# Conditional weight splits as one branch per engine, queued behind the features, in a linear-attention and mixture-of-experts kernel

## The chip, the cores and the metric

The kernel runs on one core of a Trainium2 chip. The metric is the device time of one execution in microseconds (us). Engines: PE multiplies matrices and transposes, ACT applies functions and copies, DVE does elementwise work, POOL issues the gathers and scatters, SP issues the weight loads. Each engine takes its instructions in the order in which they are queued, and waits for another engine by semaphores.

## What is computed

A layer norm and linear attention with softmax features, then a layer norm and a mixture of 8 experts of which each token takes one, over 2048 tokens of width 512 (hidden width 1792). The change touches the second half:

```python
logits = xf @ w_gate
topk_idx = jnp.argsort(-logits, axis=-1)[:, :K]          # K = 1
gates = _softmax(topk_val, axis=-1)
for e in range(E):                                        # E = 8
    mask = (topk_idx == e)
    w = (gates * mask).sum(-1, keepdims=True)
    h = _silu(xf @ w1[e]) @ w2[e]
    out = out + w * h
```

All of it is in float32. A product of two float32 matrices is made of three passes over numbers that are split into a high and a low part: hi times hi, hi times lo, lo times hi (`mm3`, lines 89 to 92).

## The kernel before

Tokens are sorted by expert into blocks of 128. The second half runs units, one after the other, each for one expert:

- `unit0` (line 1263): the first block, of the expert with the most tokens in the first half. Its second product and the building of the block tables overlap.
- `pair(q)` (line 1323): two blocks, 256 tokens. Pairs 1 and 2 are always there; 3 to 8 stand in branches (line 1502) that are entered when there are enough blocks. Here pairs 1 to 4 run.
- `wide(w, hooks)` (line 1187): 288 tokens of one expert, twice, with the single blocks 0 and 1 (`single(r)`, line 1387) behind them.
- `single(r)`: one block of 128. Singles 2 to 7 stand in branches; here 2 and 3 run.

**Weights.** An expert has 7 chunks of 128 x 2048 numbers, 1 MB each: chunks 0 to 2 and half of 3 hold `w1`, the rest of 3 and 4 to 6 hold `w2`. SP loads a chunk to `raw[c]`. It is then split: ACT copies it to `whi[c]` (`hi_piece`, line 229; the copies are recorded at line 84), and DVE subtracts that from `raw[c]` to give `wlo[c]` (`lo_piece`, recorded at line 235). Either is done in halves of 128 x 1024. `split_chunk` does both halves, hi, lo, hi, lo. When both are done, `raw[c]` is loaded again for a later unit (`load`, or `fetch` in a branch on SP).

**Conditions.** A unit of the same expert as the one before needs no new weights. So `fls[u]` (a register on ACT and on DVE, from `load_fl`, line 1131) says whether unit u must split, and `flags[u]` (SP, line 1136) whether and what to load. `split(u, c)` (line 1152) has one branch, `tc.If(fls[u] > 0)`, around `split_chunk`, on two engines, and `fetch` behind it. In this run pairs 1 and 2 have the expert of unit0 and split nothing; pairs 3 and 4 and all later units have new weights.

**Steps.** A pair has 14 steps j over the hidden width. In each, PE makes g1 (12 products into `gw`), ACT the silu to `hs` and its high part, DVE its low part (both in `hA`, recorded at lines 84 and 87), and PE makes g2 of step j - 2 into `my`. `gw` is one tile of two halves, used in turn. At the end of step j the functions of `todo[j]` are called. `step(c, i, ...)` (line 1246) splits half i of chunk c, conditionally when it is for a pair, inside `with after(pin["hi"]), after(pin["lo"])`. `ahead` and `turned` norm a block of the next pair and turn its features (transposes on PE, high part on ACT, low part on DVE). A wide has the same steps with `hooks`.

**Order.** A planner at compile time chooses the order of the instructions on each engine, from their dependences and its own estimate of durations. `after(i)` (line 147) ties what is written inside it: those of its instructions that are on i's engine are queued behind i. A branch is placed as a whole, and the tie holds for a branch that is on that engine alone.

**Singles.** Each of four gemm1 groups (`mh`) is followed by a silu (line 220) and the transposes of the one before (`tr`, line 242); then come g2 (`yl` or `my`), the conditional splits of chunks 0 to 3 for the next single and, in their midst, that one's norm and transposes (line 1455). Single 1 also writes out the rows of wide 1 (`wide_out`), one tile of which lies in `raw[2]`, and refills chunks.

## Time and profile before

| | |
|---|---|
| median of 3 runs | 694.05 us (690.66 to 696.5) |
| the profiled execution | 695.41 us, span 693.7 us |
| mean granted clock of PE | 0.971 |
| attention and block tables | 0 to about 285 us of the span |
| pair 1, pair 2 | 285.1 to 338.1, to 389.3 |
| pair 3, pair 4 | to 432.6, to 476.5 |
| wide 0, single 0 | to 527.6, to 552.0 |
| wide 1, single 1 | to 600.2, to 634.1 |
| single 2, single 3 | to 665.7, to 687.3 |

The stages are read from the timeline of PE. In the timeline a row has the start, the length, the engine, the line, the operation, the tiles (out<-in), and in brackets the idle time of that engine just before and what ended it. "ACTq" and "DVEq" are the instruction sequencers of those engines: a wait for them is a wait for a branch. Lines of helpers stand for all their callers, so L84, L87 and L235 are told apart by their tiles: `hA` belongs to features of a step, `whi` and `wlo` to a split.

### The profile page before, as it was taken

What the parts mean: (1) busy time and instruction counts of PE and PEld (TensorE: products, weight loads), DVE (VectorE), ACT (ScalarE), POOL (GpSimd) and SP (SyncE); (2) the same over time, 40 slices, a digit from 0 to 9 for tenths busy, and PEclk for the clock granted to TensorE, in tenths of its full rate; (3) what the DMA queues carried; (4) which work ended last, traced back from release to release, by engine and by line L of the source; (5) the groups of instructions that cost most, each with busy time, mean ns of one, the idle gap of its engine ahead of it and who ended that gap; (6) DMA issues with size and microseconds to landing.
All of it is one profiled execution on the core that took longest, in us unless ns stands there. A gap on an engine that the chain in (4) does not pass through costs nothing. (4 is left out here: it accounts for less than half of the span.)

```text
span 693.7 us, 14767 instructions
## 1 busy us (share of the span) xinstructions
PE 641.8 (93%) x5455; PEld 566.2 (82%) x5455; DVE 454.3 (65%) x897; ACT 376.0 (54%) x674; POOL 239.0 (34%) x340
## 2 busy tenths in 40 slices
PE   9999999999999999789979899996999999949696
PEld 7888888888899987579868797895998899838484
DVE  7988877878988698613224656554658585844833
ACT  6566666675354475423234664664558386734641
POOL 5476788787165574200210200201203300142010
PEclk9999999999999999789999999999999999979989
DMA  9511111201023781660204563754645876565510
GB/s 330 189 48 47 52 57 47 62 19 32 18 78 123 276 303 64 241 258 1 66 18 134 175 242 112 254 183 152 223 159 201 296 257 222 194 255 204 193 49 19
DMA packets 25210, 101.53 MB, mean 146 GB/s; under 512 B 3326, under 2 KB 3326, under 8 KB 17056
## 3 DMA queue, kind: packets, MB, share of 16 engines
q1 hardware_dynamic: 21088, 88.15, 36.2%
q0 software_dynamic: 3888, 12.24, 5.4%
q8 instruction: 47, 0.77, 0.4%
q14 instruction: 43, 0.35, 0.1%
q10 hardware_dynamic: 144, 0.02, 0.0%
HBM read 91.98 MB, written 8.81 MB: 145 GB/s over the span
## 5 line engine op out<-in xcount | busy, mean ns | idle before, releaser
L235 DVE TENSOR_TENSOR wlo<-raw,whi 128x1024 fp32r<-128x1024 f32 (+1 forms) x130 | 151.8, 1188 | 84.7 <-ACT whi L84 80.0
L84 ACT ACTIVATE whi<-raw 128x1024 fp32r<-128x1024 f32 (+1 forms) x135 | 130.8, 999 | 34.7 <-DMA raw<-in_w_dram 17.3
L181 POOL DMA_INDIRECT out_dram<-xg,sidx x17 | 22.1, 1302 | 178.6 <-DVE xg L1239 140.8
L87 DVE TENSOR_TENSOR hA<-hs,hA 128x256 fp32r<-128x256 f32 (+1 forms) x84 | 36.3, 432 | 64.5 <-ACT hA L84 32.9
L90 PE MATMUL gw<-xhi,whi 128*128 128x256 f32 x224 | 66.6, 297 | 5.4 <-ACT hs L1373 3.4
L663 POOL TENSOR_TENSOR ph<-t,sm 128x1024 f32<-128x1024 f32 x32 | 62.1, 1940 | 19.5 <-DVE sm L661 19.3
L1373 ACT ACTIVATE hs<-gw 128x256 f32<-128x256 f32 x56 | 21.6, 385 | 85.6 <-PE gw L92 85.6
L92 PE MATMUL gw<-xhi,wlo 128*128 128x256 f32 x224 | 65.0, 290 | 2.3 <-DVEq L1153 2.3
L91 PE MATMUL gw<-xlo,whi 128*128 128x256 f32 x224 | 65.3, 292 | 0.0
L168 POOL DMA_INDIRECT xg<-hbuf,gidx x28 | 31.4, 1122 | 69.1 <-DMA out_dram<-xg,sidx 34.8
L92 PE MATMUL my<-whi,hA 128*128 128x512 f32 x122 | 49.1, 403 | 4.0 <-DVE hA L87 4.0
L660 DVE TENSOR_REDUCE sm<-t 128x64 f32<-128x1024 f32 x32 | 38.8, 1214 | 20.2 <-ACT t L655 18.3
L90 PEld LDWEIGHTS gw<-xhi,whi 128*128 128x128 f32 x224 | 44.3, 198 | 9.5 <-ACT hs L1373 4.9
L655 ACT ACTIVATE t<-t,rstd 128x1024 f32<-128x1024 f32 x32 | 36.8, 1150 | 27.3 <-DVE t L654 24.9
L90 PE MATMUL my<-whi,hA 128*128 128x512 f32 x122 | 49.1, 402 | 1.2 <-ACTq L1153 1.2
L91 PE MATMUL my<-wlo,hA 128*128 128x512 f32 x122 | 48.8, 400 | 0.4 <-DVEq L1153 0.4
L92 PEld LDWEIGHTS gw<-xhi,wlo 128*128 128x128 f32 x224 | 44.5, 199 | 2.5 <-DVEq L1153 2.5
L91 PEld LDWEIGHTS gw<-xlo,whi 128*128 128x128 f32 x224 | 44.4, 198 | 1.9
L90 PE MATMUL po<-wohi,xh 128*128 128x260 f32 x128 | 37.5, 293 | 1.3 <-DVE lg L918 1.3
L84 ACT ACTIVATE hA<-hs 128x256 fp32r<-128x256 f32 (+1 forms) x84 | 35.9, 427 | 3.1 <-ACTq L1250 0.4
L92 PE MATMUL po<-wohi,xl 128*128 128x260 f32 x128 | 36.5, 285 | 0.1
L91 PE MATMUL po<-wolo,xh 128*128 128x260 f32 x128 | 36.1, 282 | 0.0
(418 smaller groups left out, 1897.9 us busy)
## 6 DMA issues: line engine op xcount, KB each, us to landing
raw<-in_w_dram SPq DMA_DIRECT2D x63, 1024.0 KB, 5.3
xt<-in_x_dram SPq DMA_DIRECT2D x32, 256.0 KB, 2.7
hbuf<-hb SPq DMA_DIRECT2D x8, 515.0 KB, 3.5
xT<-in_xTs_dram SPq DMA_DIRECT2D x16, 256.0 KB, 2.7
phT<-in_wv_dram SPq DMA_DIRECT2D x4, 256.0 KB, 4.0
phT<-in_wqkT_dram SPq DMA_DIRECT2D x4, 256.0 KB, 4.9
phT<-in_wqkT_dram SPq DMA_DIRECT2D x2, 512.0 KB, 5.9
phT<-in_wo_dram SPq DMA_DIRECT2D x2, 512.0 KB, 7.7
```

The costliest lines, as they stand in the source:

```text
L84: return A.activation(dst, src, AF.Copy)
L87: return V.tensor_tensor(dst, src, hi.bitcast(F32), op=OP.subtract)
L90: T.matmul(ps, ahi, bhi, start=first, stop=False)
L91: T.matmul(ps, ahi, blo, start=False, stop=False)
L92: return T.matmul(ps, alo, bhi, start=False, stop=last)
L168: G.indirect_dma_start(out=dst[0:n, :], out_offset=None, in_=hbuf if col else hbuf[0:S // 2, :], in_offset=bass.IndirectOffsetOnAxis(ap=gi ...
L181: m = G.indirect_dma_start(out=out, out_offset=bass.IndirectOffsetOnAxis(ap=sidx[0:n, col:col + 1], axis=0), in_=src[0:n, 0:D], in_offset= ...
L235: return eng.tensor_tensor(lo, r, h.bitcast(F32), op=OP.subtract)
L655: pin["ex"] = A.activation(t, t, AF.Exp, scale=st[c]["rstd"])
L660: V.tensor_reduce(sm, t, AX.X, OP.add)
L663: pin["f2"] = G.tensor_tensor(ph.rearrange("p (a f) -> p a f", f=DH), t, bc(sm, DH), op=OP.mult)
L1373: A.activation(h, p, AF.Silu)
```

## The change

A split gets two branches: one on ACT with the high halves, one on DVE with the low halves, each on its own register. `step` uses the same for its half. `split` no longer fetches; `split_fetch` does both. In the diff the lines that only rename are left out:

```diff
-    fls = {}
+    fls = {ENG.Activation: {}, ENG.DVE: {}}
...
-    def split(u, c):
-        with tc.If(fls[u] > 0):
-            split_chunk(c)
+    def split(u, c, i0=0, i1=2):
+        with tc.If(fls[ENG.Activation][u] > 0):
+            for i in range(i0, i1):
+                hi_piece(c, i)
+        with tc.If(fls[ENG.DVE][u] > 0):
+            for i in range(i0, i1):
+                lo_piece(c, i)
+
+    def split_fetch(u, c):
+        split(u, c)
         fetch(u, c)
...
@@ step
                 if u is not None and u < NQ:
-                    with tc.If(fls[u] > 0):
-                        half(c, i)
+                    split(u, c, i, i + 1)
```

The tiles of a wide: norm (`tile_n`) and transposes (`tile_t`) are two functions. In `wide` the first step has a bank of its own in both wides, and each g1 is queued behind the one before:

```diff
-                p = (bank("mh") if j == w else gw[:, (j + w) % 2, :])[:, 0:WN]
+                p = (bank("mh") if j == 0 else gw[:, j % 2, :])[:, 0:WN]
...
+                    with after(pin["g1"] if j else None):
```

At the end of `unit0` one conditional split stays; the others, and the splits of chunks 5 and 6, go to pair 1:

```diff
-        for c in range(4):
+        for c in range(5):
             load(c, nx0)
-            split(1, c)
+        with after(xh), after(xl):
+            split_fetch(1, 0)
         result(0, py, xg[0])
-        with after(xh), after(pin["y"]):
-            for c in (5, 6):
-                split_hi(c)
-                split_lo(c)
...
-        for c in range(4, NW):
-            load(c, nx0)
```

In `pair` each step takes a bank from the pool of four; features stand ahead of the splits of their step, and the ties of later splits point at them; for pair 2 the features of pair 3 come a step later (d = 3):

```diff
-                turn2(q + 1, t)
+                pin["hi"], pin["lo"] = turn2(q + 1, t)
...
+        for j, (c, i) in {6: (0, 0), 7: (0, 1), 8: (1, 0), 9: (1, 1), 10: (3, 1), 11 if q == 2 else 12: (2, 0),
+                          12 if q == 2 else 13: (2, 1), 14: (3, 0)}.items():
+            todo[j].append(step(c, i, None, q + 1))
+        if q == 1:
+            for j, (c, i) in ((0, (3, 1)), (0, (1, 0)), (1, (1, 1)), (2, (4, 0)), (2, (4, 1)), (3, (2, 0)), (3, (2, 1)),
+                              (4, (5, 0)), (4, (5, 1)), (5, (6, 0)), (5, (6, 1)), (6, (3, 0))):
+                todo[j].append(step(c, i, None, q))
+        else:
+            for i in range(6):
+                todo[i].append(step(4 + i // 2, i % 2, None, q))
         if q < NP:
-            d = 2 if q == 2 else 0
+            d = 3 if q == 2 else 0
             todo[9 if q == 2 else 0].append(lambda: gather(q + 1))
-            todo[9 + d].append(lambda: ahead(0))
-            todo[10 + d].extend((lambda: turned(0), lambda: ahead(1)))
-            todo[11 + d].append(lambda: turned(1))
+            todo[9 + d].insert(0, lambda: ahead(0))
+            todo[10 + d][0:0] = [lambda: turned(0), lambda: ahead(1)]
+            todo[11 + d].insert(0, lambda: turned(1))
...
-            todo[j].extend(fs)
-        if q == 1:
-            load_fl(3, NQ)
+            todo[j] = fs + todo[j]
...
-                p = gw[:, j % 2, 0:PT]
+                p = bank("gw")[:, 0:PT]
...
+            if q == 1 and j == 1:
+                load_fl(3, NQ)
```

In `single` the unconditional splits are tied behind the silu or the features (`si`, `pin`, and h2, x2 of the tiles in single 0), and the splits for the next single go behind its transposes:

```diff
-            for c in range(2):
-                split(f + 1, c)
-            with after(g2(py, 2, jp)), after(lo2):
-                norm(own(r + 1), V)
-                turn(*single_x(r + 1))
-            for c in range(2, 4):
-                split(f + 1, c)
+            with after(pin["hi"]), after(pin["lo"]):
+                split_fetch(f + 1, 0)
+                n = norm(own(r + 1), V)
+            with after(g2(py, 2, jp)):
+                xh, xl = turn(*single_x(r + 1))
+            with after(xh), after(xl):
+                for c in range(1, 4):
+                    split_fetch(f + 1, c)
```

The hooks of pairs 1 and 2 and of the wides move the same way; each norm stands a step ahead of its transposes or in front of the split:

```diff
-    pair(1, {5: [wide_a], 10: [wide_b], 11: [wide_c]})
+    pair(1, {0: [step(5, 0)], 1: [step(5, 1, we[4]), step(6, 0)], 2: [step(6, 1, we[4])], 5: [wide_a], 8: [wide_b],
+             9: [wide_c]})
...
-    pair(2, {0: [wide_rows_of], 5: [call(wide_x, 0)], 6: [call(wide_x, 1)], 7: [call(wide_x, 2)]})
+    pair(2, {0: [call(rows, src[t], WC + t, WT[t][1]) for t in (2, 0, 1)],
+             4: [call(wide_n, 2)], 5: [call(wide_x, 2), call(wide_n, 0)], 6: [call(wide_x, 0), call(wide_n, 1)],
+             7: [call(wide_x, 1)]})
...
-        8: [step(1, 0), call(prework_late, 0)],
-        9: [step(1, 1, ew1), call(rows, xr[0], WC), call(rows, xr[2], WC + 2)],
+        8: [call(norm_late, 0), step(1, 0)],
+        9: [call(turn_late, 0), step(1, 1, ew1), call(rows, xr[0], WC), call(rows, xr[2], WC + 2)],
```

Wide 1 has the same two lines with 1 in the place of 0.

## The prediction

> **What bounds the kernel now.** I read the page first (busy shares), then the waits of PE from 280 us on, then the timeline around each wait, and last windows laid over the stages.

> ```profile
> PE 641.8 (93%) x5455; PEld 566.2 (82%) x5455; DVE 454.3 (65%) x897; ACT 376.0 (54%) x674; POOL 239.0 (34%) x340
> ```

> PE is the bound: 93% busy against 65% for DVE. All code of the change runs behind 280 us, so the question is which waits of PE there it takes away. This is the list (waits of PE by what ended them; total us, count, longest):

> ```profile
> PE mtr L246 <- ACT hs L220: 12.3, 2, 9.6
> PE my L92 <- DVE hA L87: 4.0, 3, 1.7
> ...
> PE mtr L1166 <- DVE xg L1162: 3.6, 1, 3.6
> PE gw L90 <- ACT hs L1373: 3.4, 7, 0.5
> ...
> PE gw L92 <- DVEq L1153: 2.3, 1, 2.3
> PE gw L90 <- ACTq L1153: 2.0, 2, 1.5
> PE my L90 <- ACTq L1153: 1.2, 1, 1.2
> ...
> PE mtr L1166 <- DVE xn L1162: 0.9, 1, 0.9
> PE my L91 <- DVEq L1153: 0.4, 1, 0.4
> PE mtx L197 <- DVE xn L191: 0.3, 1, 0.3
> ```

> Each wait has a second price. After some of them the granted clock is a half; windows cut to those stretches (columns: length, PE busy, PEld, DVE, ACT, POOL, granted clock, DMA share, GB/s):

> ```profile
> 287.60:297.80 10.20, 7.38 (x31) 6.79 (x32) 3.78 (x5) 1.60 (x4) 1.33 (x2) 0.50 1.01 400
> 301.20:304.70 3.50, 3.50 (x16) 3.21 (x15) 0.00 (x0) 0.00 (x0) 0.00 (x0) 0.51 1.01 419
> 362.70:366.10 3.40, 3.40 (x13) 2.82 (x11) 1.43 (x2) 1.93 (x4) 0.65 (x1) 0.50 0.28 80
> 485.60:489.00 3.40, 3.40 (x17) 3.40 (x16) 2.22 (x3) 1.90 (x4) 2.46 (x2) 0.50 0.31 60
> 615.30:625.50 10.20, 4.14 (x13) 3.46 (x14) 5.24 (x6) 5.22 (x8) 2.32 (x2) 0.50 0.98 404
> 656.20:663.10 6.90, 6.14 (x17) 5.00 (x18) 1.31 (x3) 0.60 (x1) 0.00 (x0) 0.51 0.45 153
> ```

> Half the busy time in such a stretch is lost: 3.7 and 1.7 us at the start of pair 1, 1.7 in pair 2, 1.7 in wide 0, 2.1 in single 1, 3.1 in single 2.

> **Why the waits are there.** The end of pair 3, and the place in single 1 with the longest wait (start, length, engine, line; the bracket has the idle time before and what ended it):

> ```profile
> 427.29 0.42 ACT L84 ACTIVATE hA<-hs 128x256 fp32r<-128x256 f32 x1
> 427.61 1.99 ACT L84 ACTIVATE whi<-raw 128x1024 fp32r<-128x1024 f32 x2
> ...
> 428.69 2.36 DVE L235 TENSOR_TENSOR wlo<-raw,whi 128x1024 fp32r<-128x1024 f32 x2 [1.25 <-ACT whi L84]
> 430.97 0.42 DVE L87 TENSOR_TENSOR hA<-hs,hA 128x256 fp32r<-128x256 f32 x1
> ...
> 431.44 0.50 PE L92 MATMUL my<-whi,hA 128*128 128x512 f32 x1 [1.38 <-DVE hA L87]
> ...
> 618.82 2.00 ACT L84 ACTIVATE whi<-raw 128x1024 fp32r<-128x1024 f32 x2 [10.90 <-DMA raw<-in_w_dram]
> 620.73 0.58 ACT L220 ACTIVATE hs<-mh 128x512 f32<-128x512 f32 x1
> ...
> 621.36 0.90 PE L246 MATMUL mtr<-ident,hs 128*128 128x128 f32 x3 [9.61 <-ACT hs L220]
> ```

> In the code the feature's low part (`lo_of`, hA on DVE) stands before the step's split, and the split is asked to be queued behind it. It is not: hA's high part is done at 427.71, yet DVE runs two conditional splits first and the low part only at 430.97; PE waits 1.38 us. A branch that spans two engines escapes the order. In single 1 the same escape is dearer: the conditional split of a chunk for single 2 sits on ACT ahead of the silu of the present block, waits 10.90 us for its weights, and PE stands for 9.61.

> **The change, part by part** (against the profiled execution, 695.41 us with a span of 693.7).

> *Branches per engine, behind the features, in pairs.* The number of branches on ACT and DVE stays; each now lies on one engine and can be queued. A split on DVE begins no earlier or later than now, because it waits for ACT's high part, which keeps its place. The three waits of PE for hA (4.0 us: 0.92, 1.38, 1.67) go. What a branch costs by itself shows only from above, in DVE's waits for ACT's branches where the split isn't taken:

> ```profile
> DVE hA L87 <- ACTq L1250: 28.8, 14, 2.4
> ```

> 28.8 / 14 = 2.1 us each, beside PE work: PE has no wait in the steps concerned. That wait goes too, so -2.1 us bounds one branch from below. Above: two high parts in a row, each behind its branch, take 1.99 us (427.61), no more than twice the 1.06 of one alone (482.92 below); I allow 0.1. On the path I take 0.

> The 1.67 at the end of pair 4 is not kept, for wide 0 waits behind it for something else:

> ```profile
> 482.92 1.06 ACT L84 ACTIVATE whi<-raw 128x1024 fp32r<-128x1024 f32 x1 [2.43 <-SPq L1500]
> ...
> 484.32 0.40 PE L90 MATMUL gw<-xwh,whi 128*128 128x288 f32 x1 [2.49 <-ACT hs L1201]
> ```

> Wide 0's first split on ACT waits for SP, which passes the pairs that are not run (L1500) and there collects the loads that pair 4 issued last. Their splits keep their time, so ACT comes no earlier, and PE's 2.49 grows by what it arrives sooner. Net 0 for pair 4's end. Pair 2's end loses 0.92, but its `turned(1)` moves from step 13 to 14, the last: norm 0.54, ACT's half 0.6 and DVE's 0.69 (rows of the same shape below) now stand between the transposes and pair 3's first product, with one g2 step (about 1.4 us: 43.3 us of pair 3 are 14 steps of g1 and g2) to hide them. Bounds 0 and 1.8; I take 1.0. Together 0.92 + 1.38 - 1.0 = **1.3**.

> *Separate banks.* The seven waits of gw for the silu of the previous step (3.4 us) come at steps 1 and 2, with no g2 between two g1 groups: both halves of one tile count as one. With a bank of its own for each, **3.4** goes; lower bound 0, if another tile of that pool is late.

> *Features a step earlier in pair 2.* Now:

> ```profile
> 355.74 0.69 DVE L87 TENSOR_TENSOR xwl<-mtr,xwh 128x512 fp32r<-128x512 f32 x1 [1.40 <-ACT xwh L84]
> 359.41 1.23 DVE L235 TENSOR_TENSOR wlo<-raw,whi 128x1024 fp32r<-128x1024 f32 x1 [2.98 <-ACT whi L84]
> ...
> 360.89 0.54 DVE L1162 TENSOR_SCALAR xg<-xg 128x512 f32<-128x512 f32 x1
> ...
> 361.48 0.66 PE L1166 MATMUL mtr<-ident,xg 128*128 128x128 f32 x4 [3.59 <-DVE xg L1162]
> ```

> The norm of the next tile stands behind a split. `wide_n` runs a step ahead of the transposes and in front of the split: 3.59 + 0.93 go, and the half clock of 362.7 to 366.1 with them (1.7): **6.2**. DVE then has in a step 0.42 + 1.23 + 0.69 + 0.54 = 2.88 us against about 2.8 of PE, for three steps; its low parts are needed two steps later, which covers that. `load_fl(3, NQ)` moves into pair 1 (inside the 2.98 above now); bound 0 to 1.6, hidden. The gathers change order and issue the same three requests on POOL, 34% busy: 0.

> *Start of pair 1.* Chunks 5 and 6 of the first expert are split today before pair 1, and DVE does them in one run:

> ```profile
> 285.82 4.85 DVE L235 TENSOR_TENSOR wlo<-raw,whi 128x1024 fp32r<-128x1024 f32 x4
> ...
> 286.63 0.39 PE L90 MATMUL gw<-xhi,whi 128*128 128x256 f32 x1 [1.52 <-ACTq L1153]
> ...
> 289.42 0.58 PE L92 MATMUL gw<-xhi,wlo 128*128 128x256 f32 x1 [2.29 <-DVEq L1153]
> ```

> PE waits for the branches (L1153) behind them. The change moves these eight halves, with the two loads of 1 MB behind them, to steps 0 to 2, one branch alone stays ahead, and the other conditional splits go to steps of pair 1. Gone: 1.52 + 2.29 + the other 0.47 for ACT's branch + 1.21 + 0.42 (a smaller wait for DVE's branch) = 5.9, and 3.7 + 1.7 of half clock: 11.3. New: DVE has 4.85 + 4 x 0.42 + the result's 0.75 = 7.3 us in the first four steps, in which PE has about 8.4; the chunks are first read at step 8. The moved loads feed pair 3, 100 us later. One branch of DVE may still end behind `result`. I charge 1.0 (bounds 0 and 3.8, the two waits of today): **10.3**.

> *Rows of blocks.* In the singles the conditional splits go behind the transposes of the next block, the norm goes ahead: 12.3 (9.61 the first) + 3.65 = 15.9, and 2.1 + 3.1 of half clock: 21.1. What is late next? Single 2 and single 3, windows; then DVE's split halves in single 2, the wait for its norm, and one wait of SP:

> ```profile
> 634.10:665.70 31.60, 25.12 (x110) 19.89 (x109) 20.18 (x21) 17.55 (x23) 4.59 (x4) 0.89 0.37 122
> 665.70:687.30 21.60, 21.47 (x109) 17.56 (x107) 11.47 (x14) 10.43 (x15) 3.00 (x3) 1.00 0.09 28
> ...
> L235 DVE TENSOR_TENSOR wlo<-raw,whi 128x1024 fp32r<-128x1024 f32 x14 | 16.3, 1217 | 3.0 <-ACT whi L84 3.0
> ...
> 656.96 0.87 PE L197 MATMUL mtr<-ident,xn 128*128 128x128 f32 x3 [3.65 <-DVE xn L191]
> ...
> SPq L1150 <- DMA out_dram<-raw,sidx: 11.1, 1, 11.1
> ```

> Without waits a single takes PE 21.6 us. DVE has 20.2 in a full one: almost as much, so some of its order will show. Next late is the norm if it lands behind the first conditional split (2.4 us on DVE), in two singles. SP's queue waits 11.1 us in single 1 to refill chunk 2, behind a scatter; the split that needs it goes from ahead of the third silu to behind the transposes, a g2 of five steps or more later, and what still waits there is ACT without a feature behind it. I charge 3.0 (bounds 0 and 8): **18.0**. Single 0 has its features ahead as well, but PE is busy there already: 0. In wide 1 the norm ahead saves the 0.3 of mtx.

> Sum: 1.3 + 3.4 + 6.2 + 10.3 + 18.0 + 0.3 = 39.5. 695.4 - 39.5 = 655.9. The median of the runs shown, 694.05, lies 1.4 lower, their scatter is 6; I forecast **655**.

> **The clock.** The rows say that the half clock at 287.6 follows waits of 1.52 and 0.5 us. [...]

> **Rivals.**
> 1. *The singles keep their waits in another place.* If ACT's silu still stands behind a conditional split, or DVE's chain becomes the bound at 2.4 + 1.3 us a chunk (the split and its wait for ACT), 7 x 3.7 + 4 = 30 us in a full single, about 17 of 21 come back: 672. For it: DVE's 20.2. Against: the order is now pinned on each engine.
> 2. *Pair 1 still waits for its branches.* The 10.3 come back: 666. For it: one branch remains ahead of the first product, behind `result`. Against: nothing of 4.85 us precedes it.
> 3. *The half clock has another cause than the waits.* Then the stretches at 287.6 and 301.2, which show DMA at a share of 1.01, stay at half: 655 + 5.4 = 660. Against: 362.7 has a share of 0.28.
> 4. *The change doesn't do what it says*: the planner still puts the branches first. Only banks, pair 2's norms and the moved chunks act, about 10: 685.
> 5. *Slower*: the branch itself falls on the path. By the code pairs 2 to 4 run 8 + 14 + 14 conditional halves and singles 1 and 2 eight each: 52. If PE waited 0.9 us at each for the second join, 47 us, the forecast gain and 7 more would be gone: 702. Against: in pair 3, with a branch at nearly every step, PE has 2.3 us of wait in 43.3.

> **How the numbers follow.** Forecast 0.70, rival 1 0.14, rival 2 0.06, rival 3 0.04, rival 4 0.03, rival 5 0.03. The forecast's own range: all charges at 0 and every wait of the list gone gives 648, all at their upper bounds (1.8 + 3.4 + 3.8 + 8 instead of 5.0) gives 667; rivals 1 to 3 reach to 672. So 647 to 673, which leaves out rivals 4 and 5 and a tail of rival 1. About 1% is what a measurement can tell. Faster by over 1%: 0.95; within 1%: 0.02; slower: 0.03.

> **What would show it.** Right: PE's waits for hA (L87) and for the silu of pairs gone; no half clock around 290 and 620; silus of a single never behind whi with a wait for DMA; wide 0's wait for SP still there, longer. Wrong: PE waits of several us in single 1 or 2 for L220 or the norm; a new wait at the start of pair 3 above 2 us; waits for branches at pair 1.

## The result and the profile after

The changed kernel takes 663.64 us (median of 4 runs, 662.62 to 666.36), the kernel before in the same comparison 695.27 (690.66 to 697.31): a ratio of 0.956, with a 95% interval of 0.950 to 0.962. The profiled execution took 663.39 us with a span of 661.7, against 695.41 and 693.7. The forecast was a gain of 39.5 us on the profiled execution; the gain is 32.0. The time lies inside the range and 8.6 us above the number.

The busy line of the page, and then the list of PE's waits behind 284 us (total us, count, longest). Line numbers are those of the changed kernel: L1153 and L1156 are the branches of a split on ACT and on DVE, L1513 the branch past pairs that are not run, L1207 the silu of a wide.

```profile
PE 628.7 (95%) x5455; PEld 558.4 (84%) x5455; DVE 456.3 (69%) x897; ACT 373.8 (56%) x674; POOL 239.2 (36%) x340
```

```profile
PE mtr L197 <- DVE xn L191: 5.9, 4, 3.0
PE mh L90 <- DVEq L1513: 5.1, 1, 5.1
PE my L90 <- ACTq L1153: 4.0, 1, 4.0
PE gw L90 <- ACT hs L1207: 1.0, 1, 1.0
PE gw L92 <- DVEq L1156: 0.8, 1, 0.8
...
PE my L91 <- DVEq L1156: 0.5, 1, 0.5
...
PE gw L91 <- DVE xlo L87: 0.3, 1, 0.3
```

The 12.3 us for silus of singles, the 4.0 for hA, the 3.4 for silus of pairs and the 4.5 for pair 2's norms are gone. In their place stand one wait of 4.0 for a branch of ACT, one of 5.1 for a branch of DVE (1.2 before), and 5.9 for norms (3.65 before), of which single 1 has 2.98 and single 2 has 1.81.

Where the time went shows best by stage. The stages of the table run from the end of one stage's last result on DVE to the end of the next one's (the first such end is the row at 285.70 in the timeline further down, 286.45 us); all of it is in us, and the last column is the median of the runs. The first two rows are the result, the others the experiments below. The stages come from one profiled execution each, and the clock in it is partly chance, as the last section shows: a difference of 1 or 2 us in one stage should not be read too closely.

| kernel | pair 1 | pair 2 | pair 3 | pair 4 | wide 0, single 0 | wide 1, single 1 | single 2 | single 3 | time |
|---|---|---|---|---|---|---|---|---|---|
| before | 53.17 | 51.10 | 43.27 | 43.86 | 75.28 | 82.46 | 31.48 | 21.54 | 695.27 |
| changed | 48.93 | 44.61 | 40.33 | 41.16 | 75.93 | 75.13 | 24.32 | 19.17 | 663.64 |
| loads 0, 3, 1, 2, 4 | 42.98 | 44.91 | 40.39 | 41.17 | 76.83 | 75.14 | 25.92 | 19.12 | 659.29 |
| chunks 5, 6 later | 42.91 | 44.90 | 40.30 | 41.14 | 77.09 | 75.15 | 24.33 | 18.48 | 658.23 |
| norm first | 49.19 | 44.60 | 40.30 | 41.14 | 75.47 | 72.63 | 24.68 | 18.18 | 656.51 |
| one branch for two engines | 49.40 | 45.54 | 49.45 | 48.21 | 74.06 | 76.97 | 28.47 | 21.59 | 686.29 |
| singles' block undone | 48.61 | 44.60 | 40.30 | 41.14 | 76.07 | 84.59 | 30.24 | 21.59 | 679.74 |
| before + branches | 53.15 | 50.30 | 41.89 | 42.12 | 78.98 | 85.41 | 30.19 | 21.53 | 694.05 |
| before + banks | 49.04 | 53.99 | 46.31 | 45.53 | 76.15 | 83.83 | 30.23 | 21.57 | 699.98 |
| before + both | 49.98 | 50.03 | 40.42 | 40.51 | 78.20 | 85.42 | 30.21 | 21.54 | 689.50 |
| chunk 2 early | 48.34 | 44.61 | 39.70 | 41.13 | 76.84 | 75.11 | 25.89 | 19.24 | 663.36 |
| four edits | 45.19 | 44.90 | 39.75 | 41.13 | 72.80 | 72.64 | 22.54 | 18.83 | 651.77 |
| three edits | 42.94 | 44.89 | 39.70 | 41.13 | 71.61 | 72.63 | 22.19 | 18.21 | 646.65 |

From wide 1 on the change gains 7.33 + 7.16 + 2.37 = 16.9 us; forecast were 18.3. Singles 2 and 3 are best read together: in the changed kernel DVE makes single 2's result at 636.12, behind a split, though PE has begun single 3 at 632.76; before, the two came at 665.76 and 665.56. Pair 1 gains 4.24 where 10.3 and a quarter of the banks' 3.4 were forecast, 11.2 together. The missing 7 us are almost all there. This is its start in the changed kernel, from the timeline:

```profile
285.70 0.75 DVE L1245 SCALAR_TENSOR_TENSOR xg<-my,xg 128x512 f32<-128x512 f32 x1 [1.60 <-PE my L1272]
...
289.29 1.06 ACT L84 ACTIVATE whi<-raw 128x1024 fp32r<-128x1024 f32 x1 [0.25 <-ACTq L1153]
...
291.18 2.00 ACT L84 ACTIVATE whi<-raw 128x1024 fp32r<-128x1024 f32 x2
...
293.81 1.04 ACT L84 ACTIVATE whi<-raw 128x1024 fp32r<-128x1024 f32 x1
...
294.95 0.80 PE L90 MATMUL my<-whi,hA 128*128 128x512 f32 x1 [4.00 <-ACTq L1153]
...
296.22 0.80 PE L91 MATMUL my<-wlo,hA 128*128 128x512 f32 x1 [0.48 <-DVEq L1156]
```

The four halves of chunks 5 and 6 (1.06 + 2.00 + 1.04 us on ACT) stand ahead of the branch for the second half of chunk 3. That half holds the weights of the first second-product. The branch isn't taken (the timeline has no split of that half), and still PE stands 4.00 us for it: it goes on at 294.95, 0.10 us after the last of the four halves ends (293.81 + 1.04). The clock then falls. Below are that stretch and the one with the wait for the norm in single 1 (columns as before: length, the engines' busy time, granted clock, DMA share, GB/s):

```profile
294.30:301.10 6.80, 5.67 (x19) 4.69 (x20) 1.81 (x3) 0.55 (x1) 1.04 (x1) 0.50 1.01 422
...
600.00:611.80 11.80, 9.07 (x42) 7.56 (x43) 10.10 (x11) 6.96 (x8) 0.57 (x1) 1.00 0.96 345
```

Half of 5.67 us is 2.8. With 4.00 and 0.48 this makes 7.3 us at the start of pair 1.

### The profile page after: what moved, and what is told of

Its sections match the earlier page's. It is cut to its first block, busy times and chain, and to the rows that moved or that the text cites. A ratio compares the mean times of both kernels' runs of the same rounds, so it can differ in the third digit from the quotient of the medians.

```text
span 661.7 us, 14720 instructions
## 1 busy us (share of the span) xinstructions
PE 628.7 (95%) x5455; PEld 558.4 (84%) x5455; DVE 456.3 (69%) x897; ACT 373.8 (56%) x674; POOL 239.2 (36%) x340
## 5 line engine op out<-in xcount | busy, mean ns | idle before, releaser
L235 DVE TENSOR_TENSOR wlo<-raw,whi 128x1024 fp32r<-128x1024 f32 (+1 forms) x130 | 151.5, 1189 | 36.8 <-ACT whi L84 35.1
L84 ACT ACTIVATE whi<-raw 128x1024 fp32r<-128x1024 f32 (+1 forms) x135 | 130.2, 998 | 7.4 <-DMA raw<-in_w_dram 4.1
L87 DVE TENSOR_TENSOR hA<-hs,hA 128x256 fp32r<-128x256 f32 (+1 forms) x84 | 36.6, 435 | 81.0 <-ACT hA L84 47.3
L181 POOL DMA_INDIRECT out_dram<-xg,sidx x17 | 20.6, 1211 | 148.9 <-DVE xg L1245 131.9
L90 PE MATMUL gw<-xhi,whi 128*128 128x256 f32 x224 | 64.6, 288 | 0.0
L92 PE MATMUL gw<-xhi,wlo 128*128 128x256 f32 x224 | 63.6, 284 | 0.8 <-DVEq L1156 0.8
L91 PE MATMUL gw<-xlo,whi 128*128 128x256 f32 x224 | 63.7, 284 | 0.3 <-DVE xlo L87 0.3
L90 PE MATMUL my<-whi,hA 128*128 128x512 f32 x122 | 49.1, 403 | 4.0 <-ACTq L1153 4.0
L660 DVE TENSOR_REDUCE sm<-t 128x64 f32<-128x1024 f32 x32 | 38.9, 1214 | 20.2 <-ACT t L655 18.3
L91 PE MATMUL my<-wlo,hA 128*128 128x512 f32 x122 | 48.6, 398 | 0.5 <-DVEq L1156 0.5
L92 PE MATMUL my<-whi,hA 128*128 128x512 f32 x122 | 48.5, 398 | 0.0
L91 PEld LDWEIGHTS gw<-xlo,whi 128*128 128x128 f32 x224 | 42.8, 191 | 2.2 <-DVE xlo L87 0.5
L90 PEld LDWEIGHTS gw<-xhi,whi 128*128 128x128 f32 x224 | 42.8, 191 | 2.2 <-ACT xhi L84 0.4
L92 PEld LDWEIGHTS gw<-xhi,wlo 128*128 128x128 f32 x224 | 42.8, 191 | 1.0 <-DVEq L1156 1.0
L90 PE MATMUL po<-wohi,xh 128*128 128x260 f32 x128 | 37.5, 293 | 1.2 <-DVE lg L918 1.2
L84 ACT ACTIVATE hA<-hs 128x256 fp32r<-128x256 f32 (+1 forms) x84 | 35.8, 427 | 2.5
L92 PE MATMUL po<-wohi,xl 128*128 128x260 f32 x128 | 36.5, 285 | 0.1
L91 PE MATMUL po<-wolo,xh 128*128 128x260 f32 x128 | 36.1, 282 | 0.0
```

The costliest lines, as they stand in the source:

```text
L84: return A.activation(dst, src, AF.Copy)
L87: return V.tensor_tensor(dst, src, hi.bitcast(F32), op=OP.subtract)
L90: T.matmul(ps, ahi, bhi, start=first, stop=False)
L91: T.matmul(ps, ahi, blo, start=False, stop=False)
L92: return T.matmul(ps, alo, bhi, start=False, stop=last)
L181: m = G.indirect_dma_start(out=out, out_offset=bass.IndirectOffsetOnAxis(ap=sidx[0:n, col:col + 1], axis=0), in_=src[0:n, 0:D], in_offset= ...
```

## The experiments

### The branch behind the moved halves

Theory: a branch that isn't taken still lets PE go on only when the work ahead of it on its engine has ended. Two kernels take that work away in different ways. The first alters the order of the loads, by which the branch of chunk 3 comes to stand ahead of the halves of chunk 5:

```diff
-        for c in range(5):
+        for c in (0, 3, 1, 2, 4):
             load(c, nx0)
```

> The changed kernel with one line of unit0 altered: the five loads for the next unit are issued in the order 0, 3, 1, 2, 4 instead of 0, 1, 2, 3, 4. The branch for the second half of chunk 3 then stands ahead of the halves of chunk 5 on ACT; in the changed kernel it stands behind the halves of chunks 5 and 6. Theory (PE's 4.00 us at 290.95 is the branch's place behind the moved halves: its event comes at 294.88, when the last of them ends): the 4.00 and the 0.48 behind it go, and the half clock of 294.3 to 301.1 with them (about 6.1 us of busy time in it, half lost, 3.1): 7.5 us together, 656. Rival A (the half clock follows the DMA share, which is 1.01 there): the waits go, the half clock stays, about 659. Rival B (each branch costs this much wherever it stands): no change, 663.

The second leaves the loads and moves the halves:

```diff
-    pair(1, {0: [step(5, 0)], 1: [step(5, 1, we[4]), step(6, 0)], 2: [step(6, 1, we[4])], 5: [wide_a], 8: [wide_b],
+    pair(1, {3: [step(5, 0)], 4: [step(5, 1, we[4])], 5: [wide_a, step(6, 0)], 6: [step(6, 1, we[4])], 8: [wide_b],
```

> The changed kernel with the unconditional halves of chunks 5 and 6 moved from steps 0 to 2 of pair 1 to steps 3 to 6 (loads as in the changed kernel, so chunk 3's load still lands at about 298.5). Theory (work queued ahead of the branch): nothing stands ahead of the branch of chunk 3 but features, PE's wait at its first second-product is below 0.5 us, no half clock: 656, as with the other order of loads. Rival A (the branch waits for the landing of chunk 3's load): PE waits till 298.5, 7 us instead of 4: 667. Rival B (half clock follows the DMA share): about 659.

They take 659.29 us (ratio to before 0.951, 0.945 to 0.957) and 658.23 (0.951, 0.945 to 0.958). Pair 1 falls to 42.98 and 42.91 us, 6.0 less than in the changed kernel. The rest of what was expected is lost later: wide 0 with single 0 is 0.9 and 1.2 us longer, and single 2 of the first kernel 1.6 us. The waits of the second at wide 0's start, where pair 4 now ends earlier and SP's collection of its loads does not:

```profile
PE gw L90 <- ACT hs L1207: 4.8, 1, 4.8
PE mh L90 <- DVEq L1513: 1.6, 1, 1.6
```

The timeline of the same kernel at the start of pair 1, where the branch stands behind a feature only:

```profile
290.22 0.42 ACT L84 ACTIVATE hA<-hs 128x256 fp32r<-128x256 f32 x1
...
290.74 0.49 PE L90 MATMUL my<-whi,hA 128*128 128x512 f32 x1 [0.96 <-ACTq L1153]
```

Again PE goes on 0.10 us after the end of the ACT work ahead of the branch. The landing of chunk 3's load isn't what is waited for: its place among the loads is the same as in the changed kernel, and the wait is 0.96 instead of 4.00. The kernel with the other load order answers the question of the clock; its window is the same stretch as above:

```profile
294.30:301.10 6.80, 5.83 (x37) 4.90 (x36) 2.13 (x4) 2.34 (x7) 0.85 (x1) 1.00 1.02 423
```

The DMA share is 1.02 here and 1.01 there, the clock 1.00 here and 0.50 there. The half clock followed the wait, not the transfers: the third rival of the prediction falls.

### The norm behind the first conditional split

```diff
-                split_fetch(f + 1, 0)
                 n = norm(own(r + 1), V)
+            with after(n):
+                split_fetch(f + 1, 0)
```

> The changed kernel with the norm of the next single ahead of the first conditional split in singles 1 and later (that split is tied behind the norm). Theory (PE's 2.98 and 1.81 us for xn are the 2.36 us of low halves queued before the norm on DVE): both go, DVE has 20.3 of 24.3 us busy in single 2 and can be 0.6 later with its first split: 4.8 us less, 659. Rival (DVE's chain of splits is the bound in a single, and the time reappears at the next first product): a gain below 1 us, 663.

It takes 656.51 us (0.947, 0.941 to 0.953; 655.25 to 658.97). First the timeline of the changed kernel, then that of this one, both in single 1:

```profile
599.76 2.36 DVE L235 TENSOR_TENSOR wlo<-raw,whi 128x1024 fp32r<-128x1024 f32 x2 [0.54 <-ACT whi L84]
602.04 0.54 DVE L191 TENSOR_SCALAR xn<-xg 128x512 f32<-128x512 f32 x1
602.73 0.63 PE L197 MATMUL mtr<-ident,xn 128*128 128x128 f32 x4 [2.98 <-DVE xn L191]
```

```profile
597.86 0.54 DVE L191 TENSOR_SCALAR xn<-xg 128x512 f32<-128x512 f32 x1
598.32 2.35 DVE L235 TENSOR_TENSOR wlo<-raw,whi 128x1024 fp32r<-128x1024 f32 x2
```

Counted from the end of single 0's result, the split begins at 62.2 us here and at 62.4 in the changed kernel, so it loses nothing, and the norm no longer waits for it. The two waits of 2.98 and 1.81 are gone; in the profiled execution wide 1 with single 1 gains 2.5 us, singles 2 and 3 together only 0.6, because single 2 has a new wait of 1.73 us for a silu at 612.66 (PE L246 <- ACT L220). The median gains 7.1, more than the 4.8 of the waits; runs of this kernel spread over 3.7 us, and what lies above 4.8 is not explained.

### One branch over two engines, with everything else as changed

```diff
-        with tc.If(fls[ENG.Activation][u] > 0):
-            for i in range(i0, i1):
-                hi_piece(c, i)
-        with tc.If(fls[ENG.DVE][u] > 0):
+        with tc.If(fls[u] > 0):
             for i in range(i0, i1):
-                lo_piece(c, i)
+                half(c, i)
```

> The changed kernel with one branch over ACT and DVE for each conditional split, as before the change; places, ties and banks stay as changed. Theory of the prediction (a branch that spans two engines escapes the order): pairs have the waits for features back (4.0 us of hA, less what wide 0's wait for SP takes, about 2.5), and the singles theirs (17 us): about 683. Rival (in the singles it is the place and the tie that count; in this kernel's list of ACT the silus stand ahead of the conditional splits as in the changed one): singles as in the changed kernel, only pairs lose: 664 to 668.

It takes 686.29 us (0.989, 0.986 to 0.992): 22.7 us of the change's gain hang on the kind of branch. But the loss isn't where the theory put it. Pairs 3 and 4 lose 9.1 and 7.1 us and become slower than before the change; from wide 1 on only 8.4 of 16.9 are lost. The start of pair 3 in its timeline:

```profile
385.98 0.41 ACT L84 ACTIVATE hA<-hs 128x256 fp32r<-128x256 f32 x1
386.12 2.47 DVE L235 TENSOR_TENSOR wlo<-raw,whi 128x1024 fp32r<-128x1024 f32 x2 [5.58 <-ACT whi L84]
...
388.51 0.76 DVE L87 TENSOR_TENSOR hA<-hs,hA 128x256 fp32r<-128x256 f32 x2
...
388.98 0.50 PE L92 MATMUL my<-whi,hA 128*128 128x512 f32 x1 [2.74 <-DVE hA L87]
```

Two conditional halves run on DVE ahead of the features of steps 0 and 1, and PE stands 2.74 us for them. In the kernel before, with the same kind of branch, this wait didn't exist at a pair's start; why it does now is told by the banks below.

### The block of the singles undone

```diff
-            with after(pin["hi"]), after(pin["lo"]):
-                split_fetch(f + 1, 0)
-                n = norm(own(r + 1), V)
-            with after(g2(py, 2, jp)):
-                xh, xl = turn(*single_x(r + 1))
-            with after(xh), after(xl):
-                for c in range(1, 4):
-                    split_fetch(f + 1, c)
+            for c in range(2):
+                split_fetch(f + 1, c)
+            with after(g2(py, 2, jp)), after(lo2):
+                norm(own(r + 1), V)
+                turn(*single_x(r + 1))
+            for c in range(2, 4):
+                split_fetch(f + 1, c)
```

> The changed kernel with one block undone: in singles 1 and later the conditional splits stand where they stood before the change (two of them ahead of the next block's norm and transposes, untied, two behind), each still with one branch per engine. Theory (in the singles it is the place and the tie, not the kind of branch): ACT's silus stand behind conditional splits again, wide 1, single 1, 2 and 3 take as long as before the change (82.5, 31.5 and 21.5 us between results instead of 75.1, 24.3 and 19.2), 16.9 us more: 680. Rival (two branches are enough for ACT to run silus in time): below 668.

It takes 679.74 us (0.979, 0.972 to 0.985), as the theory said; wide 1 to single 3 are 17.8 us longer than in the changed kernel by the profile. The timeline of ACT in single 1:

```profile
603.30 2.00 ACT L84 ACTIVATE whi<-raw 128x1024 fp32r<-128x1024 f32 x2 [11.07 <-DMA raw<-in_w_dram]
605.21 0.58 ACT L220 ACTIVATE hs<-mh 128x512 f32<-128x512 f32 x1
```

The split has its own branch on ACT and stands ahead of the silu all the same, waiting 11.07 us for its weights. In singles it is the place that costs this wait, not the kind of branch.

### Branches alone, banks alone, both

Three kernels put parts of the change into the kernel before. Branches alone (`half` here under two branches, as in the diff of the change):

```diff
-                    with tc.If(fls[u] > 0):
-                        half(c, i)
+                    with tc.If(fls[ENG.Activation][u] > 0):
+                        hi_piece(c, i)
+                    with tc.If(fls[ENG.DVE][u] > 0):
+                        lo_piece(c, i)
```

> The kernel before with one part of the change: each conditional split has one branch on ACT and one on DVE; places, ties and banks as before the change. Theory (pairs lose time by the kind of branch, singles by the place): singles as before; in pairs 3 and 4 the features are free of the two-engine branch, 1.4 us each at the tails plus what half clock follows, pair 2 about 1: 3 to 5 us less than before, about 690. Rival (the kind of branch is the whole gain): 675 or less. Rival (twice as many branches cost by themselves): slower than before, above 696.

Banks alone:

```diff
-        gw = psw.tile([P, 2, 512], F32, name="gw", tag="w")
...
-                p = gw[:, j % 2, 0:PT]
+                p = bank("gw")[:, 0:PT]
```

> The kernel before with one part of the change: each step of a pair takes a bank of its own from the pool of four instead of half of one tile of two banks. Prediction's term: 3.4 us less, 0.85 in each pair, 691. Rival (in pair 1 and at the tails PE waits for branches and features instead): 1 us or less.

And both edits in one kernel:

> The kernel before with two parts of the change: one branch per engine and banks of their own in pairs; places and ties as before. Alone they were worth 0.25% less time and 0.73% more. Theory (separate banks let PE and the silus run ahead, and only a split whose branch lies on one engine stays behind the features, so each needs the other): pairs 3 and 4 take 40.3 and 41.1 us as in the changed kernel, with the rest as in the kernel with the branches alone: about 688, 1% less than before. Rival (the two add up): 0.5% slower, 699.

Branches alone give 694.05 us (0.998, 0.994 to 1.001): no difference that can be told. Banks alone give 699.98 (1.007, 1.004 to 1.011): slower. Both give 689.50 (0.991, 0.988 to 0.995). The waits of PE, first with branches alone, then with banks alone:

```profile
PE mtr L246 <- ACT hs L220: 12.3, 2, 9.6
...
PE gw L90 <- ACT hs L1379: 3.5, 7, 0.6
```

```profile
PE my L92 <- DVE hA L87: 9.6, 5, 2.9
```

The start of pair 3 with banks alone shows the same order as in the kernel with one branch for two engines:

```profile
392.17 2.47 DVE L235 TENSOR_TENSOR wlo<-raw,whi 128x1024 fp32r<-128x1024 f32 x2 [3.81 <-DMA raw<-in_w_dram]
...
395.03 0.50 PE L92 MATMUL my<-whi,hA 128*128 128x512 f32 x1 [2.73 <-DVE hA L87]
```

With branches alone the wait for hA is gone, but the seven waits for a shared tile stay, and the singles' 12.3 us stay to the last tenth. Pairs 3 and 4 gain 1.4 and 1.7 us, as expected, but wide 0 with single 0 and wide 1 with single 1 lose 3.7 and 3.0. With banks alone the waits for the shared tile are gone, and the wait for hA grows from 4.0 to 9.6: PE and the silu of the next step run ahead, and the two-engine splits slip in front of the features that are now wanted earlier. With both, pairs 3 and 4 (385 to 466 us) show this one wait in the whole list, where the kernel before (390.17 to 477.30 us) has the two lines behind it:

```profile
PE gw L90 <- PEq L1505: 1.1, 1, 1.1
```

```profile
PE my L92 <- DVE hA L87: 3.0, 2, 1.7
PE gw L90 <- ACT hs L1373: 1.9, 4, 0.5
```

Pairs 3 and 4 take 40.42 and 40.51 us, as in the changed kernel, and no part of them is at half clock in this kernel or in the one before. The two edits do not add up: each needs the other. Pair 1 is also shorter, by 4.13 us with banks alone and 3.19 with both, but it has 6.8 us at half clock in these two traces and 13.7 in that of the kernel before; how much of it the banks bring is not shown. Part of what the four pairs gain with both (10.5 us by the table) is given back in wide 0 with single 0 and wide 1 with single 1, 2.9 and 3.0 us. These stages have 13.7 us at half clock, and so with branches alone, where the kernel before has 3.4 (without what follows single 1's silu wait, which all of them have), so much of what is given back is clock.

### The start of wide 0, and the edits together

In the changed kernel PE starts wide 0 with 5.07 us of wait for DVE's branch past the pairs that are not run, and 3.4 us at half clock behind it (464.95 to 468.36). Then it waits 0.98 for the silu of step 1, which stands on ACT behind a split that waits for SP's collection of the last two loads of pair 4. The timeline of the changed kernel, and the wait for DVE's branch in the kernel before:

```profile
470.25 1.06 ACT L84 ACTIVATE whi<-raw 128x1024 fp32r<-128x1024 f32 x1 [0.92 <-SPq L1513]
...
471.65 0.40 PE L90 MATMUL gw<-xwh,whi 128*128 128x288 f32 x1 [0.98 <-ACT hs L1207]
```

```profile
PE mh L90 <- DVEq L1500: 1.2, 1, 1.2
```

One edit lets one of these loads go a step earlier:

```diff
-        for j, (c, i) in {6: (0, 0), 7: (0, 1), 8: (1, 0), 9: (1, 1), 10: (3, 1), 11 if q == 2 else 12: (2, 0),
-                          12 if q == 2 else 13: (2, 1), 14: (3, 0)}.items():
+        for j, (c, i) in {6: (0, 0), 7: (0, 1), 8: (1, 0), 9: (1, 1), 10: (3, 1), 11: (2, 0),
+                          12: (2, 1), 14: (3, 0)}.items():
```

> The changed kernel with one edit: the split of chunk 2 in pairs 3 and later at steps 11 and 12 instead of 12 and 13. Theory (wide 0 starts when SP has collected the last two loads of pair 4, which share the bandwidth): the first of the two leaves about 2 us sooner, the last lands sooner, and wide 0 with single 0 takes 72 to 74 us instead of 75.9: 660 to 661. [...]

It takes 663.36 us (0.953, 0.949 to 0.956): no change, where the theory had 660 to 661. Its waits:

```profile
PE mtr L197 <- DVE xn L191: 5.8, 4, 3.0
PE mh L90 <- DVEq L1513: 5.8, 1, 5.8
PE my L90 <- ACTq L1153: 4.0, 1, 4.0
```

The 1.0 for the silu is gone, and the branch of DVE takes 5.8. Two more kernels put the edits together.

> The changed kernel with four edits together: the halves of chunks 5 and 6 at steps 3 to 6 of pair 1, the loads of unit0 in the order 0, 3, 1, 2, 4, the norm ahead of the first conditional split in singles 1 and later, and the split of chunk 2 in pairs 3 and later at steps 11 and 12 instead of 12 and 13, so that its load leaves a step earlier. Theory: the first two together 6 to 7 us (PE's remaining 1.0 us for the branch of chunk 3 goes as well), the norm 4 to 5, and wide 0's 4.8 us for SP, which collects the last two loads of pair 4, shrinks by about 2 as one of them starts 2.9 us sooner: 650. Rival (wide 0's wait is set by the very last load alone, or other work at the end of pair 4 suffers): 652 to 654.

It takes 651.77 us (0.938, 0.931 to 0.946). Three of its four executions lie between 650.78 and 652.34; the fourth took 1567.57, has no trace and is not explained. Pair 1 is at 45.19, not at 42.9. Its timeline says why:

```profile
296.53 1.04 ACT L84 ACTIVATE whi<-raw 128x1024 fp32r<-128x1024 f32 x1
...
297.67 0.50 PE L90 MATMUL my<-whi,hA 128*128 128x512 f32 x1 [1.91 <-ACTq L1153]
```

The other load order has put a half of chunk 5 ahead of a later branch, and for the third time PE goes on 0.10 us after that half ends. So the last kernel takes the load order back:

> As the kernel with four edits, but with the loads of unit0 back in the order 0, 1, 2, 3, 4; three edits are left: chunks 5 and 6 later, norm first, chunk 2 a step earlier. In the kernel with four, PE waits 1.91 us at 295.75 for a branch of ACT that stands behind a half of chunk 5, and the clock is low after it. Theory (an untaken branch is passed only when the engine's earlier work has ended): in the order of this kernel only a feature stands ahead of the first such branch, pair 1 takes 42.9 us as in the kernel with those halves alone moved, not 45.2: 649.5. Rival (the load order is what counts, or the time is lost again at wide 0's wait for SP): 651 to 652.

It takes 646.65 us (0.931, 0.927 to 0.934), 7% less than before and 17 us less than the changed kernel. Its busy line and what is left of PE's waits:

```profile
PE 625.3 (97%) x5455; PEld 555.3 (86%) x5455; DVE 454.7 (71%) x897; ACT 373.8 (58%) x674; POOL 247.2 (38%) x340
```

```profile
PE gw L90 <- ACT hs L1207: 1.4, 1, 1.4
PE mh L90 <- DVEq L1514: 1.2, 1, 1.2
PE mtr L197 <- DVE xn L191: 1.1, 2, 0.5
PE my L90 <- ACTq L1153: 1.0, 1, 1.0
```

Chunk 2's edit is worth nothing by itself, but wide 0 with single 0 is 5.5 us shorter here (71.61 against 77.09 with the halves of chunks 5 and 6 moved alone; the norm's edit, the other difference, is worth 0.5 there by itself). PE had waited 4.8 us for the silu behind SP and now waits 1.4; 6.8 us at half clock behind that wait (462.0 to 468.8) are gone as well. Which of the two waits ends last differs from kernel to kernel, since PE's wait for DVE's branch lies between 0.6 and 5.8 us where there is one. Why it does so was not found.

## Why the prediction was right and where it failed

The time fell inside the range. The singles and pair 2 gained in the way that was forecast, though for the singles one reason was wrong. Of the 7.5 us that are missing, 6.9 are in pair 1.

*The step that failed is "Start of pair 1".* It gave 10.3 us after a charge of 1.0, with bounds 0 and 3.8, and looked for a late branch on DVE behind `result`. That one came, at 0.76 us. What was missed is ACT: eight halves were moved "to steps 0 to 2" and counted as hidden behind PE's 8.4 us, and the branches of the steps were taken to cost nothing. But the four on ACT, 4.1 us, landed ahead of a branch whose join the second product waits for. The charge should have been 0.76 + 4.00 + 0.48 + 2.8 of half clock, 8.0 us; 11.3 less this, with 0.85 for the banks, gives 4.1, and 4.24 were measured. The upper bound of 3.8 left the clock out, though the prediction had named it as every wait's second price. With this work out of the way pair 1 takes 42.91 us, 10.3 less than before; 11.2 were forecast. Rival 2, that pair 1 still waits for its branches, came in part: 6.0 of its 10.3 us. It looked at the one branch ahead of the first product and was put low because "nothing of 4.85 us precedes it"; 4.1 us on ACT preceded a later one.

*Separate banks*: the waits went, as forecast, but the term of 3.4 was no term of its own. Alone the edit makes the kernel 4.2 us slower (699.98 against 695.81 in its comparison). Its lower bound of 0 excluded a loss without a reason. *Pairs' tails* (1.3): the branches alone are worth nothing that can be measured, and without them the changed kernel loses 22.7 us. In pairs 3 and 4 the two terms were 0.85 + 1.38 and 0.85 + 1.67 us, and both edits together give 2.85 and 3.35 there. The sum was about right, but its parts were priced as if each stood alone, so that is luck. The charge for `turned(1)` was 1.0 and is 0.34 (the wait for xlo).

*Pair 2* (6.2 with the norms ahead): the waits for norms are gone, and the stage gains 6.49, of which branches and banks by themselves give 1.07. By subtraction 5.4 are left for the norms. No run moves the norms alone, and the kernel with branches and banks has no half clock in pair 2 where the one before has 3.4 us of it, so the size is known only roughly; the mechanism is right.

*Singles* (18.0; its own terms, 21.1 less 3.0, make 18.1): 17.8 us come back when this block alone is undone. The charge of 3.0 was put at the right place, the norm behind the first conditional split, and measured 2.98 + 1.81. That the wait of 2.98 cost no clock on top in the profiled execution was luck: in the kernel with the other load order it did, as the last section shows. One reason was wrong: the prediction blamed the branch over two engines for the silu's wait. With a branch per engine in the old place the wait is there (11.07 us on ACT); with one branch over both in the new place no wait for a silu is left, though 8.4 us are lost: PE waits 9.0 us for DVE there instead of 4.8, and 10.2 us are at half clock that the changed kernel ran at full. Both parts are needed.

*Wide 0* (0 for pair 4's end, so that pair 4 and wide 0 together gain the 0.85 of the banks): pair 4 gains 2.70 and wide 0 with single 0 loses 0.65, together 2.05. The reason was wrong: the wait for SP was to grow from 2.49 by what PE arrives sooner and shrank to 0.98, and the wait for DVE's branch, which the prediction did not name, grew from 1.2 to 5.07.

*The clock* (rival 3): shown false by the equal DMA shares above. Rivals 1, 4 and 5 did not come; the undone block of the singles is what rival 1 would have looked like.

*The signs.* Of the signs of being right, the waits for hA and for the silus of pairs are gone and no silu of a single waits for weights. There is no half clock at 620, but there is at 294 to 301, and the wait for SP is shorter, not longer. Of the signs of being wrong, waits for branches in pair 1 and a norm wait of 2.98 in single 1 came.

## What to carry to other kernels

A branch that isn't taken was not free here: PE, which needed its result, went on 0.10 us after the work ahead of it on its engine had ended, and waited up to 4.00 us for that work. So ask of work that is moved into "hidden" slots not only whether it is hidden, but which joins come behind it on the same engine. Price parts of a change by themselves only where one doesn't set the order of the other: here two edits were worth nothing and a loss alone, and a gain together.

## What the runs showed of the hardware

The release of PE came 0.10 us after the end of the ACT work ahead of an untaken branch in three kernels, with waits of 4.00, 1.91 and 0.96 us.

The clock did not go by the length of a wait. PE's wait of 1.91 us at 295.75 in the kernel with four edits was followed by half clock; the wait of 2.98 us at 599.75 in the changed kernel was not; and the same wait of 2.98 us, at 594.30 in the kernel with the other load order, was.

```profile
598.07:601.48 3.41, 1.68 (x8) 1.06 (x6) 2.87 (x5) 2.05 (x3) 1.94 (x2) 1.00 0.94 324
601.48:604.89 3.41, 2.16 (x12) 1.89 (x13) 1.79 (x3) 1.49 (x3) 0.00 (x0) 1.00 0.88 315
```

```profile
594.57:597.98 3.41, 0.70 (x5) 0.69 (x6) 2.57 (x3) 0.69 (x2) 1.80 (x1) 1.00 0.93 335
597.98:601.40 3.42, 3.42 (x10) 2.67 (x9) 2.57 (x3) 3.42 (x5) 0.00 (x0) 0.50 0.89 285
```

```profile
295.55:298.96 3.41, 1.50 (x8) 1.05 (x7) 2.51 (x3) 1.75 (x3) 0.00 (x0) 1.00 0.98 410
298.96:302.38 3.42, 3.42 (x16) 3.23 (x15) 0.00 (x0) 0.24 (x1) 0.00 (x0) 0.50 0.95 337
```

The wait of 599.75 to 602.73 is shared by two windows, and in both PE is busy for over 1.6 us (the clock behind them is full, as the stretch from 600.00 to 611.80 above shows); the same wait at 594.30 lies almost whole in one, which keeps 0.70. Of all windows at full clock behind 284 us in the thirteen traces, the 55 with PE busy for 1.50 us or less were each followed by half clock, and none with more than 1.81 was; of the 31 in between 8 were. The edges lie elsewhere in each trace (one at 284.04 in the changed kernel, at 285.46 with chunk 2 early), so whether a wait of 2 or 3 us costs clock is partly chance.

DVE's branch past the pairs that are not run held PE for 0.6 to 5.8 us in twelve of the thirteen traces. What sets that length was not found.
